# First transfers of a fused RWKV, soft-MoE and bilinear kernel put in another order, with four fewer warming matmuls

## The chip, the cores and the metric

The kernel runs on one core of a Trainium2 chip. The metric is the device time of one execution in microseconds, taken as the median of several runs.

## What is computed

Three layers follow one another in float32. The first is a linear attention with a decay per key channel (4 batches, 8 heads, 768 positions, 48 channels), the second a soft mixture of 8 experts with 4 slots each, the third a bilinear layer.

```python
def _attn_ref(r, k, v, w, u):
    state = np.zeros((B, H, D, D), dtype=np.float32)
    for t in range(S):
        kt, vt, rt, wt = (k[:, :, t], v[:, :, t], r[:, :, t], w[:, :, t])
        cur = np.einsum('bhd,bhe->bhde', u[None] * kt, vt)
        y[:, :, t] = np.einsum('bhd,bhde->bhe', rt, state + cur)
        state = wt[:, :, :, None] * state + np.einsum('bhd,bhe->bhde', kt, vt)

def _moe_ref(x, phi, w1, w2):            # x: 3072 x 384, 32 slots, inner width 1024
    logits = x @ phi
    slot_input = softmax_over_tokens(logits).T @ x
    for e in range(E):
        slot_out[e] = np.maximum(slot_input[e] @ w1[e], 0.0) @ w2[e]
    return softmax_over_slots(logits) @ slot_out

def _moe2_ref(x, w_a, w_b, w_out):       # inner width 1536
    return ((x @ w_a) * (x @ w_b)) @ w_out
```

The three matrices of the last layer are stored in float64. The kernel turns them into float32 with integer operations on ScalarE, VectorE and GpSimd.

## The kernel before

**Units.** The attention is cut into 16 units (`NU`). A unit is four heads over 384 positions of one batch, and the 384 positions are three chunks of 128. Units 0 and 1 are the two halves of the heads over the same positions, and so are 2 and 3, and so on. For every unit four inputs are loaded: w (the decays), k, r and v. `Chunked.load` (line 481) issues one such load as three DMAs on SyncE's queue, one for each chunk, 96 KB each, in pieces of 48 floats. SyncE issues its DMAs strictly in the order of the program, and a DMA whose destination is still being read waits there, with all that come behind it. In the text w1 means the decays of unit 1, k2 the keys of unit 2, and so on.

**Buffers.** w, k and r have one buffer each (`self.nat`), so the load for the next unit may start only when this unit has been turned; v has three. `front` (line 492) prepares a unit: `turn` (501) transposes w, k and r on TensorE, in two halves p = 0 and 1, and ScalarE copies them out of PSUM (L510 for w, L512 for k and r). `decays` (528) multiplies the decays up by a scan on VectorE (L529), `ends` takes a reciprocal (L538), `backward` (532) scans from the other end (L534), `key` and `query` multiply these into k and r (L547, L551). At the end of `turn` for k and r, and in `over` (541) for w, the load for unit n + 1 is issued into the buffer that has just become free. `over` itself is a ScalarE pass over w that sums how far it exceeds 1 (L543).

**A unit's second part.** `mid` (565) makes the masked scores: matmuls L579, masked on VectorE (L583). It turns the keys back (L591), updates the states (L599 on TensorE, L604 and L610 on VectorE) and makes the bonus term (L628 and after). `out` (662) makes the result of the unit (L672, L680, L683).

**Order of the work.** The schedule is written by hand: the order of the calls is the order on each engine. In the main loop over n (from line 1392) `run_all` weaves five streams by weights: `mid` of unit n, `front` of unit n + 1, `out` of unit n − 1, a piece of the expert layer, and a piece of `convert` (730), which makes float32 of the float64 matrices. The weaving places the turn of w for unit n + 1 between the key turn and the scores of unit n, and in the first round of `convert` two `stage` calls (701; ScalarE L704 and L705) come between the two halves p = 0 and p = 1 of the turn of w for unit 2.

**The start.** Fourteen matmuls on zeros (`WARM`, L1353) run on TensorE while the first loads are on their way. `Chunked.__init__` (426) issues w0, k0, r0, v0, the small tensor u and v1; `build_consts` (155) issues phi (L157); the front of unit 0 issues k1, w1, r1. Four float64 pieces of 384 KB (L723) are first loaded when `convert` is first called, in round 1 of the loop, behind v2. Later pieces follow one by one. Expert weights are loaded on the same queue (L773).

**The end.** After the attention the expert layer waits for its weights, and the bilinear layer follows; the change does not touch these.

Of the kernel before, what the change touches and what calls it, by code (L numbers as in the profile page):

```python
# [26 lines left out]
KEEP = (0, 0, 0, 0, 0, 0, 0, 0, 0, 0, 0, 0, 2, 4, 10, 2)  # L27
KEPT = 1
MOEW = (327, 327, 300, 200, 400, 0, 400)
WARM = 14  # L30
LATER = {6: 'more', 7: 'half', 9: 'more', 10: 'half'}
FEND = 0.53
CONV0 = 1
# [110 lines left out]
        self.NG = self.NT // self.G  # L144


def build_ident(nc, pool):
    ident = pool.tile([128, 128], F32, name="ident")
    nc.gpsimd.memset(ident, 1.0)
    nc.gpsimd.affine_select(out=ident, in_=ident, compare_op=ALU.is_equal, fill=0.0,  # L150
                            base=0, channel_multiplier=1, pattern=[[-1, 128]])
    return {"ident": ident}


def build_consts(nc, pool, sh, phi, k):
    phi_sb = pool.tile([128, sh.KB, sh.NS], F32, name="phi_sb")
    nc.sync.dma_start(out=phi_sb, in_=phi.rearrange("(k p) s -> p k s", p=128))  # L157
    k["phi"] = phi_sb
    ident = k["ident"]
    NS = sh.NS  # L160
    same = pool.tile([3 * NS, 4, NS], F32, name="same")
    for i in range(4):
        nc.gpsimd.tensor_copy(out=same[:, i, :], in_=ident[0:3 * NS, 0:NS])
    for i in range(1, 3):
        nc.gpsimd.tensor_copy(out=same[i * NS:(i + 1) * NS, :, :], in_=same[0:NS, :, :])
    k["same"] = same.rearrange("p c s -> p (c s)")
    half = pool.tile([128, 1], F32, name="half")
    nc.gpsimd.memset(half, 1.0)
    nc.gpsimd.memset(half[0:32], 0.5)
    k["half"] = half  # L170
    ones = pool.tile([128, 1], F32, name="ones")
    nc.gpsimd.memset(ones, 1.0)
    k["ones"] = ones
    zero = pool.tile([128, 1], F32, name="zero")
    nc.gpsimd.memset(zero, 0.0)
    k["zero"] = zero
# [233 lines left out]
class Chunked:  # L410
# [15 lines left out]
    def __init__(self, nc, sb, pool, sh, k, r, kk, v, w, u):  # L426
        self.nc, self.sh, self.k = nc, sh, k
        self.src = {"r": r, "k": kk, "w": w, "v": v}
        D = sh.D
        N = 6 * (C + 1)  # L430
        NP = sh.H // 2
        mask = sb.tile([128, C], F32, name="mask")
        nc.gpsimd.memset(mask, 1.0)
        nc.gpsimd.affine_select(out=mask, in_=mask, compare_op=ALU.is_gt, fill=0.0,
                                base=0, channel_multiplier=-1, pattern=[[1, C]])
        self.mask = mask
        lo = sb.tile([128, N // 2], F32, name="lo")
        nc.gpsimd.memset(lo, PLOW)
        nc.gpsimd.memset(lo[:, 0:N // 2:C + 1], 1.0)
        self.lo = lo  # L440
        neg1 = sb.tile([128, 1], F32, name="neg1")
        nc.vector.memset(neg1, -1.0)
        nc.scalar.activation(out=sb.tile([128, 1], F32, tag="neg"), in_=neg1, func=ACTF.Copy)
        self.neg1 = neg1
        self.nat = {}
        for nm, nb in (("w", 1), ("k", 1), ("r", 1), ("v", 3)):
            W = D if nm == "v" else 64
            self.nat[nm] = [sb.tile([128, 3, 4, W], F32, name="nat_" + nm + (str(i) if nm == "v" else ""))
                            for i in range(nb)]
            for t in self.nat[nm]:  # L450
                if W > D:
                    nc.gpsimd.memset(t[:, :, :, D:], 1.0 if nm == "w" else 0.0)
        for nm in "wkr":
            self.load(nm, 0)
        self.load("v", 0)
        u2 = sb.tile([128, NP, 32], F32, name="u2")
        nc.gpsimd.memset(u2, 0.0)
        uv = u.rearrange("(q hh) d -> hh d q", hh=2)
        for hh in range(2):
            nc.sync.dma_start(out=u2[64 * hh:64 * hh + D, :, hh], in_=uv[hh])  # L460
        self.u2 = u2
        self.load("v", 1)
        self.wt = sb.tile([128, N + 1], F32, name="wt")
        nc.gpsimd.memset(self.wt[:, 0:N + 1:C + 1], 0.0)
        self.d1 = sb.tile([128, N], F32, name="dl")
        nc.gpsimd.memset(self.d1, 0.0)
        self.sbd = [sb.tile([128, 2, 3, 2 * D], F32, name="sbd") for i in range(2)]
        for t in self.sbd:
            nc.gpsimd.memset(t, 0.0)
        nu = sh.NG * 2  # L470
        self.pc_all = pool.tile([128, nu, 6], F32, name="pc_all")
        self.wover = pool.tile([128, nu], F32, name="wover")
        self.T = [[sb.tile([128, 2, 3, D], F32, name="T") for i in range(2)] for q in range(2)]
        self.st = {}

    def unit(self, n):
        g, q = divmod(n, 2)
        b, hf = divmod(g, 2)
        return b, hf, q

    def load(self, nm, n):
        nc, D, G = self.nc, self.sh.D, self.sh.G
        if n >= 2 * self.sh.NG:
            return
        b, hf, q = self.unit(n)
        t = self.nat[nm][n % len(self.nat[nm])]
        for c in range(3):
            s = hf * G + c * C
            nc.sync.dma_start(out=t[:, c, :, 0:D],  # L489
                              in_=self.src[nm][b, 4 * q:4 * q + 4, s:s + C, :].rearrange("h p d -> p h d"))  # L490

    def front(self, n, sb, ps_t):
# [6 lines left out]
        pc = self.pc_all[:, n, :]  # L499

        def turn(nm, p):
            t = self.nat[nm][n % len(self.nat[nm])]
            pt = ps_t.tile([128, 3, C], F32, tag="tp", name="pt")
            for c in range(3):
                nc.tensor.transpose(out=pt[:, c, :],  # L505
                                    in_=t[:, c, 2 * p:2 * p + 2, :].rearrange("p h d -> p (h d)"),
                                    identity=ident)
            off = p * 3 * C
            if nm == "w":
                nc.scalar.activation(out=part(wt, p, 1), in_=pt, func=ACTF.Copy)  # L510
            else:
                nc.scalar.activation(out=(kT if nm == "k" else rT)[:, off:off + 3 * C],  # L512
                                     in_=pt.rearrange("p c s -> p (c s)"), func=ACTF.Copy)
            if p and nm != "w":
                self.load(nm, n + 1)
# [23 lines left out]
            nc.gpsimd.tensor_copy(out=pc, in_=P[:, C::C + 1])  # L539

        def over():
            t = self.nat["w"][0].rearrange("p c h d -> p (c h) d")[:, :, 0:self.sh.D]
            nc.scalar.activation(out=t, in_=t, func=ACTF.Relu, bias=self.neg1, accum_out=self.wover[:, n:n + 1])  # L543
            self.load("w", n + 1)

        def key(p):
            (nc.gpsimd if n else nc.vector).tensor_tensor(out=part(suf, p, 1), in0=part(suf, p, 1), in1=plain(kT, p),  # L547
# [182 lines left out]
def convert(nc, sb, jobs, n):  # L730

    raws = [load_f64(nc, sb, src, n) for src, _ in jobs[:RAWS]]
    stage(nc, jobs[0][1], raws[0])
    for i, (_, dst) in enumerate(jobs):
        if i + 1 < len(jobs):
# [457 lines left out]
def kernel(  # L1193
# [145 lines left out]
    with tc.manual_schedule(), ExitStack() as fast:  # L1339
# [49 lines left out]
        conv = convert(nc, sb, js, NH)  # L1389
        nconv = 4 * len(js)  # L1390
        early = wq.loads(NPRE)
        for n in range(NU + 1):
            streams = []
            if n < NU:
# [45 lines left out]
    with tc.If(val > 0):  # L1440
        with ExitStack() as slow:
# [8 lines left out]
                sb.add(slots.take(i), *Chunked.AREAS[i - NPRE])  # L1450
            k = build_ident(nc, pool)
            build_consts(nc, pool, sh, phi, k)
            moe = Moe(nc, pool, dp, sh, k)
            sb2 = Carve()
            siT = k["phi"]
# [48 lines left out]
```

## Time and profile before

| what | value |
|---|---|
| median of 3 runs | 389.91 us (389.46 to 389.98) |
| the profiled execution's own time | 389.08 us |
| its span, first to last instruction | 387.4 us |
| mean granted TensorE clock | 0.944 |
| busy: TensorE, VectorE, ScalarE, GpSimd | 87%, 78%, 59%, 46% of the span |
| moved by DMA | 73.75 MB, mean 190 GB/s |

The profile is of one execution. PE is TensorE's matmul part and PEld its weight load, DVE is VectorE, ACT ScalarE, POOL GpSimd, SP SyncE; a q behind a name is the queue of the engine, where it issues. Times count from the start of the span, which is 1.7 us shorter than the execution's own time. L505 is line 505 of the program printed above. The chain of waits follows the work back from the last instruction, each time to what released it.

### The profile page before, as it was taken

How to read it: one execution, taken by the hardware profiler on the slowest of the kernel's cores; microseconds unless marked ns; L12 is line 12 of the kernel's file. 1: busy time of each engine (PE TensorE's matmuls, PEld its weight loads, DVE VectorE, ACT ScalarE, POOL GpSimd, SP SyncE). 2: the span in 40 equal slices, each digit the busy share in tenths (PEclk: the TensorE clock that was granted, in tenths of full speed). 3: DMA queues.
4: the chain of work that ended last, by engine and by line, in shares of the span. 5: the costliest groups of instructions: out<-in, count | busy, mean ns of one | idle time of the engine just before them, and what ended most of it. 6: DMA issues, size and time to landing. Idle time of an engine off the chain costs nothing.

```text
span 387.4 us, 9985 instructions
## 1 busy us (share of the span) xinstructions
PE 336.3 (87%) x3634; PEld 265.7 (69%) x3634; DVE 303.2 (78%) x616; ACT 226.8 (59%) x672; POOL 179.3 (46%) x224
## 2 busy tenths in 40 slices
PE   8587979988878979878879888899998988999993
PEld 4365867766757858757757776654357867999993
DVE  2476999999999998999999995343519879887851
ACT  3275786785976958877768775234313235544451
POOL 5263766666675666765757761000006834222200
PEclk9697789999999879989989999899999999999998
DMA  7759687889979767989686989599929400899422
GB/s 124 126 111 267 152 195 209 185 164 237 243 148 236 172 129 201 225 198 213 153 174 155 240 278 311 192 330 377 368 81 217 92 0 2 229 277 301 146 89 70
DMA packets 138634, 73.75 MB, mean 190 GB/s; under 512 B 105328, under 2 KB 133104, under 8 KB 138576
## 3 DMA queue, kind: packets, MB, share of 16 engines
q1 hardware_dynamic: 137424, 69.48, 71.6%
q0 software_dynamic: 1152, 3.54, 2.8%
q8 instruction: 31, 0.51, 0.6%
q14 instruction: 27, 0.22, 0.2%
HBM read 67.68 MB, written 5.31 MB: 188 GB/s over the span
## 4 chain that ended last, share of the span: by engine, by line
DVE 51%; PE 23%; DMA 12%; issue 5%; SPq 4%; ACT 3%; POOL 0%; DVEq 0%; ACTq 0%; POOLq 0%
DVE s L534 8%; DVE s L529 8%; DMA s<-in_moe_w_dram 6%; DVE s L583 6%; PE yo L1103 6%; DVE s L712 5%; DVE s L551 4%; DVE wab L714 4%; PE tp L968 3%; PE yo L1106 3%; SPq L489 3%; DVE s L683 2%; DVE wo L714 2%; DVE s L610 2%; PE tp L579 2%
## 5 line engine op out<-in xcount | busy, mean ns | idle before, releaser
L505 PE MATMUL tp<-ident,s 128*128 128x128 f32 x288 | 49.5, 295 | 7.3 <-ACT s L593 3.6
L579 PE MATMUL tp<-s,s 64*128 64x128 f32 x384 | 38.6, 304 | 17.8 <-DVE s L610 9.5
L579 PEld LDWEIGHTS tp<-s,s 64*128 64x128 f32 x384 | 31.1, 201 | 23.1 <-issue 20.8
L554 POOL TENSOR_TENSOR s<-s,s 128x384 f32<-128x384 f32 x32 | 37.4, 1187 | 18.5 <-DVE s L551 18.5
L647 ACT ACTIVATE s<-s,s 128x48 f32<-128x48 f32 x192 | 45.6, 323 | 0.2
L505 PEld LDWEIGHTS tp<-ident,s 128*128 128x128 f32 x288 | 33.2, 147 | 17.3 <-issue 5.3
L547 POOL TENSOR_TENSOR s<-s,s 128x384 f32<-128x384 f32 x30 | 36.7, 1236 | 15.8 <-DVE s L534 10.0
L529 DVE TENSOR_TENSOR_SCAN s<-s,s 128x387 f32<-128x387 f32 x32 | 33.1, 1072 | 7.2 <-ACT s L510 7.2
L583 DVE TENSOR_TENSOR s<-tp,s 128x384 f32<-128x384 f32 x64 | 32.4, 545 | 7.8 <-PE tp L579 7.6
L1103 PE MATMUL yo<-s,s 128*128 128x384 f32 x192 | 38.1, 339 | 0.3 <-DVE s L1068 0.3
L534 DVE TENSOR_TENSOR_SCAN s<-s,s 128x387 f32<-128x387 f32 x32 | 35.0, 1121 | 0.5
L680 PEld LDWEIGHTS y<-s,s 128*64 128x64 f32 x768 | 29.0, 156 | 9.1 <-issue 8.8
L1103 PEld LDWEIGHTS yo<-s,s 128*128 128x128 f32 x192 | 33.7, 188 | 1.5 <-DVE s L1068 0.9
L680 PE MATMUL y<-s,s 128*64 128x48 f32 x768 | 33.3, 243 | 0.0
L512 ACT ACTIVATE s<-tp 128x384 f32<-128x384 f32 x64 | 30.2, 489 | 1.6 <-PE tp L505 0.6
L717 POOL TENSOR_TENSOR wab<-wab,s 128x384 int32<-128x384 int32 x24 | 27.9, 1160 | 6.3 <-DVE wab L714 2.8
L968 PE MATMUL tp<-s,s 128*128 128x384 f32 x144 | 27.3, 343 | 3.5 <-DVE s L954 3.2
L968 PEld LDWEIGHTS tp<-s,s 128*128 128x128 f32 x144 | 24.5, 188 | 7.1 <-DVE s L954 4.5
L1110 ACT ACTIVATE s<-yo 128x384 f32<-128x384 f32 x24 | 11.8, 493 | 27.8 <-PE yo L1107 14.4
L712 DVE TENSOR_SCALAR s<-s 128x384 uint32<-128x384 uint32 x36 | 23.2, 644 | 3.1 <-ACT wab L704 3.1
L1111 POOL DMA_DIRECT2D out_dram<-s x18 | 9.9, 550 | 33.8 <-ACT s L1110 31.9
L620 POOL TENSOR_TENSOR s<-s,pc_all 64x288 f32<-64x288 f32 (+1 forms) x32 | 21.2, 662 | 6.6 <-DVE s L610 5.4
(190 smaller groups left out, 733.0 us busy)
## 6 DMA issues: line engine op xcount, KB each, us to landing
s<-in_moe_w_dram SPq DMA_DIRECT2D x64, 384.0 KB, 6.1
s<-in_w_dram SPq DMA_DIRECT2D x48, 96.0 KB, 3.7
s<-in_k_dram SPq DMA_DIRECT2D x48, 96.0 KB, 4.6
s<-in_r_dram SPq DMA_DIRECT2D x48, 96.0 KB, 3.5
s<-in_v_dram SPq DMA_DIRECT2D x48, 96.0 KB, 3.4
s<-in_moe_w_a_dram SPq DMA_DIRECT2D x12, 384.0 KB, 4.1
s<-in_moe_w_b_dram SPq DMA_DIRECT2D x12, 384.0 KB, 3.6
s<-in_moe_w_out_dram SPq DMA_DIRECT2D x12, 384.0 KB, 3.6
```

The lines of the kernel that those rows point to most:

```text
L505: nc.tensor.transpose(out=pt[:, c, :], in_=t[:, c, 2 * p:2 * p + 2, :].rearrange("p h d -> p (h d)"), identity=ident)
L529: nc.vector.tensor_tensor_scan(out=P[:, hs[p]], data0=wt[:, hs[p]], data1=self.lo, initial=0.0, op0=ALU.mult, op1=ALU.max)
L534: nc.vector.tensor_tensor_scan(out=suf[:, hs[p]][:, ::-1], data0=wt[:, o + 1:o + H + 1][:, ::-1], data1=d1[:, hs[p]][:, ::-1], initial=0.0 ...
L547: (nc.gpsimd if n else nc.vector).tensor_tensor(out=part(suf, p, 1), in0=part(suf, p, 1), in1=plain(kT, p), op=ALU.mult)
L554: nc.gpsimd.tensor_tensor(out=plain(rT, p), in0=plain(rT, p), in1=plain(kT, p), op=ALU.mult)
L579: nc.tensor.matmul(out=aps[hh][:, c, :], lhsT=K[64 * hh:64 * hh + 64, o + 1:o + 1 + C], rhs=R[64 * hh:64 * hh + 64, o:o + C], start=True, ...
L583: nc.vector.tensor_tensor(out=a, in0=aps[hh], in1=self.mask.unsqueeze(1).to_broadcast([128, 3, C]), op=ALU.mult)
L647: nc.scalar.activation(out=av[:, c, h], in_=V[:, c, h, 0:D], func=ACTF.Copy, scale=a0[:, c, h // 2, h % 2:h % 2 + 1])
L680: nc.tensor.matmul(out=yp[th, c, hh, :], lhsT=am[p, hh][:, c, th], rhs=V[:, c, 2 * p + hh, :], start=False, stop=c == 2 and hh == 1)
L712: nc.vector.tensor_scalar(out=raw[:, :, 1], in0=raw[:, :, 1], scalar1=0x80000000, scalar2=None, op0=ALU.bitwise_and)
L968: nc.tensor.matmul(out=tp[m], lhsT=a[:, m * 128:(m + 1) * 128], rhs=b, start=first and i == 0, stop=last and i == 2)
L1103: nc.tensor.matmul(out=y, lhsT=a[:, m, :], rhs=self.th[:, m, :], start=m == 0 and a is fh, stop=False)
```

## The change

Five edits, all at the start of the program:

- The decays of unit 1 get a place of their own, `self.second`, in one of the two buffers that carry the tag "x", and are loaded right behind r0. `tile` says which place a unit's input has. GpSimd sets the unused columns of the new place (one more memset).
- `over` issues the load of w for unit n + 1 only from n = 2 on. The load of w2 is written ahead of the main loop, into the old buffer.
- `convert` gets a `yield` behind its first four loads, and is stepped once ahead of the main loop, so these four loads (384 KB each) stand in front of w2, k2, r2 and v2.
- v1 is issued behind the front of unit 0, phi behind w2.
- 10 warming matmuls in place of 14.

```diff
-WARM = 14
+WARM = 10
...
+def load_phi(nc, phi, k):
+    nc.sync.dma_start(out=k["phi"], in_=phi.rearrange("(k p) s -> p k s", p=128))
...
+        self.second = sb.tile([128, 3, 4, 64], F32, tag="x", name="nat_w1")
+        nc.gpsimd.memset(self.second[:, :, :, D:], 1.0)
         for nm in "wkr":
             self.load(nm, 0)
+        self.load("w", 1)
         self.load("v", 0)
...
-        self.load("v", 1)
...
+    def tile(self, nm, n):
+
+        return self.second if nm == "w" and n == 1 else self.nat[nm][n % len(self.nat[nm])]
...
-            t = self.nat["w"][0].rearrange("p c h d -> p (c h) d")[:, :, 0:self.sh.D]
+            t = self.tile("w", n).rearrange("p c h d -> p (c h) d")[:, :, 0:self.sh.D]
             nc.scalar.activation(out=t, in_=t, func=ACTF.Relu, bias=self.neg1, accum_out=self.wover[:, n:n + 1])
-            self.load("w", n + 1)
+            if n > 1:
+                self.load("w", n + 1)
...
     raws = [load_f64(nc, sb, src, n) for src, _ in jobs[:RAWS]]
+    yield 0
     stage(nc, jobs[0][1], raws[0])
...
         early = wq.loads(NPRE)
+        att.load("v", 1)
+        next(conv)
+        att.load("w", 2)
+        load_phi(nc, phi, k)
         for n in range(NU + 1):
```

`load` and `turn` now ask `tile` for the place, and `build_consts` only makes phi's buffer.

On SyncE's queue, the first loads before. A row is one load; in `s_2_76<-in_w_dram` the left side is the buffer and the right side the input.

```order
L489 DMA s_2_76<-in_w_dram 128x4x48 x3
L489 DMA s_2_79<-in_k_dram 128x4x48 x3
L489 DMA s_3_80<-in_r_dram 128x4x48 x3
L489 DMA s_6_92<-in_v_dram 128x4x48 x3
L460 DMA s_7_93<-in_u_dram 48x4x1 x2
L489 DMA s_3_83<-in_v_dram 128x4x48 x3
L157 DMA phi_sb<-in_moe_phi_dram 128x3x32
L489 DMA s_2_79<-in_k_dram 128x4x48 x3
L489 DMA s_2_76<-in_w_dram 128x4x48 x3
L489 DMA s_3_80<-in_r_dram 128x4x48 x3
```

The same place in the changed program:

```order
L497 DMA s_2_76<-in_w_dram 128x4x48 x3
L497 DMA s_2_79<-in_k_dram 128x4x48 x3
L497 DMA s_3_80<-in_r_dram 128x4x48 x3
L497 DMA s_7_93<-in_w_dram 128x4x48 x3
L497 DMA s_6_92<-in_v_dram 128x4x48 x3
L465 DMA s_7_93<-in_u_dram 48x4x1 x2
L497 DMA s_2_79<-in_k_dram 128x4x48 x3
L497 DMA s_3_80<-in_r_dram 128x4x48 x3
L497 DMA s_3_83<-in_v_dram 128x4x48 x3
```

w1 moved from ninth to fourth place, into the buffer `s_7_93`, and v1 went behind r1; phi left this part.

Still on SyncE's queue, the loads that follow, before (in_moe_w_a is the first float64 matrix, in_moe_w the expert weights):

```order
L489 DMA s_2_79<-in_k_dram 128x4x48 x3
L489 DMA s_2_76<-in_w_dram 128x4x48 x3
L489 DMA s_3_80<-in_r_dram 128x4x48 x3
L489 DMA s_4_87<-in_v_dram 128x4x48 x3
L723 DMA s_1_72<-in_moe_w_a_dram 128x768
L723 DMA s_1_73<-in_moe_w_a_dram 128x768
L723 DMA s_1_74<-in_moe_w_a_dram 128x768
L723 DMA s_1_75<-in_moe_w_a_dram 128x768
L773 DMA s_9_391<-in_moe_w_dram 128x3x256
```

And now:

```order
L732 DMA s_1_72<-in_moe_w_a_dram 128x768
L732 DMA s_1_73<-in_moe_w_a_dram 128x768
L732 DMA s_1_74<-in_moe_w_a_dram 128x768
L732 DMA s_1_75<-in_moe_w_a_dram 128x768
L497 DMA s_2_76<-in_w_dram 128x4x48 x3
L148 DMA phi_sb<-in_moe_phi_dram 128x3x32
L497 DMA s_2_79<-in_k_dram 128x4x48 x3
L497 DMA s_3_80<-in_r_dram 128x4x48 x3
L497 DMA s_4_87<-in_v_dram 128x4x48 x3
L783 DMA s_9_388<-in_moe_w_dram 128x3x256
```

The four float64 pieces went ahead of everything of unit 2, w2 went ahead of k2, and phi stands behind w2. On TensorE, VectorE, ScalarE and GpSimd the order of the work stays as it was, apart from the four matmuls less and the one memset more.

## Rows read from the trace of the kernel before

**Rows 1.** Busy time in stretches: us, busy (instructions) of PE, PEld, DVE, ACT, POOL; PEclk, DMA share, GB/s.

```profile
40.00:230.00 190.00, 164.94 (x2136) 132.50 (x2135) 185.31 (x378) 143.78 (x473) 125.87 (x134) 0.94 0.84 195
230.00:258.00 28.00, 24.39 (x331) 18.09 (x330) 13.33 (x51) 12.06 (x48) 2.65 (x7) 0.94 0.81 265
```

**Rows 2.** What VectorE waited for, 0 to 40 us: total, times, longest.

```profile
DVE s L529 <- ACT s L510: 7.2, 2, 6.7
DVE s L583 <- PE tp L579: 6.6, 2, 4.8
DVE s L712 <- ACT wab L704: 3.1, 1, 3.1
```

**Rows 3.** The chain of waits, 10 to 37 us: start, length, what.

```profile
13.26 3.19 DMA s<-in_w_dram
...
28.21 3.92 DMA s<-in_moe_w_a_dram
```

**Rows 4.** Timeline of SyncE's queue: start, length, instruction; x3 are a load's three DMAs.

```profile
2.40 1.61 SPq L489 DMA_DIRECT2D s<-in_k_dram  x3
...
7.41 0.92 SPq L460 DMA_DIRECT2D s<-in_u_dram  x2
8.38 1.54 SPq L489 DMA_DIRECT2D s<-in_v_dram  x3
...
28.21 1.93 SPq L723 DMA_DIRECT2D s<-in_moe_w_a_dram  x4
```

**Rows 5.** Timeline of TensorE, 0 to 36 us; the wait ahead of a row in brackets.

```profile
1.26 5.69 PE L1353 MATMUL tp<-s 128*128 128x512 bf16 x14 [1.26 <-DVE s L442]
...
6.79 2.26 PE L505 MATMUL tp<-ident,s 128*128 128x128 f32 x18
...
18.48 1.54 PE L505 MATMUL tp<-ident,s 128*128 128x128 f32 x6
...
26.03 0.30 PE L505 MATMUL tp<-ident,s 128*128 128x128 f32 x1
...
27.38 0.33 PE L505 MATMUL tp<-ident,s 128*128 128x128 f32 x1 [0.26 <-DMA s<-in_w_dram]
```

**Rows 6.** Timeline of ScalarE, 16 to 36 us.

```profile
27.75 0.49 ACT L510 ACTIVATE s<-tp 128x384 f32<-128x384 f32 x1 [0.79 <-PE tp L505]
32.15 0.54 ACT L704 ACTIVATE wab<-s 128x384 f32<-128x384 f32 x1 [3.91 <-DMA s<-in_moe_w_a_dram]
...
33.99 0.46 ACT L510 ACTIVATE s<-tp 128x384 f32<-128x384 f32 x1
```

**Rows 7.** Timeline of VectorE, 16 to 36 us.

```profile
18.58 1.02 DVE L583 TENSOR_TENSOR s<-tp,s 128x384 f32<-128x384 f32 x2 [4.85 <-PE tp L579]
...
28.61 1.02 DVE L583 TENSOR_TENSOR s<-tp,s 128x384 f32<-128x384 f32 x2 [1.77 <-PE tp L579]
32.72 0.36 DVE L712 TENSOR_SCALAR s<-s 128x384 uint32<-128x384 uint32 x1 [3.09 <-ACT wab L704]
33.00 0.96 DVE L529 TENSOR_TENSOR_SCAN s<-s,s 128x387 f32<-128x387 f32 x1
34.48 0.96 DVE L529 TENSOR_TENSOR_SCAN s<-s,s 128x387 f32<-128x387 f32 x1 [0.53 <-ACT s L510]
```

**Rows 8.** The four float64 loads from 28.2 to 29.7 us, issue to landing.

```profile
DMA to landing us min/median/max: 3.9/5.0/6.2
```

**Rows 9.** DMA issues of 20 to 28.2 us: count, KB each, median us to landing.

```profile
s<-in_w_dram SPq DMA_DIRECT2D x3, 96.0 KB, 3.0
```

**Rows 10.** The DMA issued from 31.1 to 31.2 us, the same columns.

```profile
s<-in_k_dram SPq DMA_DIRECT2D x1, 96.0 KB, 6.5
```

**Rows 11.** Busy time in stretches, the columns of rows 1.

```profile
13.50:14.00 0.50, 0.00 (x0) 0.00 (x0) 0.24 (x1) 0.47 (x1) 0.50 (x1) 0.50 0.81 158
20.00:26.00 6.00, 5.04 (x66) 3.94 (x66) 5.79 (x14) 5.71 (x21) 2.98 (x4) 1.00 0.48 90
31.00:31.50 0.50, 0.50 (x6) 0.40 (x4) 0.00 (x0) 0.00 (x0) 0.00 (x0) 1.00 0.94 369
```

**Rows 12.** The chain of waits, 225 to 262 us: the same twelve matmuls, twice.

```profile
232.07 1.31 PE y L672 x12
...
241.56 2.49 PE y L672 x12
```

More of the change, by code (lines that the diff above doesn't have):

```diff
@@ L155, in build_consts @@
 def build_consts(nc, pool, sh, phi, k):
-    phi_sb = pool.tile([128, sh.KB, sh.NS], F32, name="phi_sb")
-    nc.sync.dma_start(out=phi_sb, in_=phi.rearrange("(k p) s -> p k s", p=128))
-    k["phi"] = phi_sb
+    k["phi"] = pool.tile([128, sh.KB, sh.NS], F32, name="phi_sb")
     ident = k["ident"]
@@ L485, in load @@
         b, hf, q = self.unit(n)
-        t = self.nat[nm][n % len(self.nat[nm])]
+        t = self.tile(nm, n)
         for c in range(3):
@@ L501, in turn @@
         def turn(nm, p):
-            t = self.nat[nm][n % len(self.nat[nm])]
+            t = self.tile(nm, n)
             pt = ps_t.tile([128, 3, C], F32, tag="tp", name="pt")
@@ L1452 @@
             build_consts(nc, pool, sh, phi, k)
+            load_phi(nc, phi, k)
             moe = Moe(nc, pool, dp, sh, k)
```

## The prediction

> **What bounds the kernel now.** I read the busy time by stretches first, then VectorE's waits, then the chain of waits and the timelines of the first 36 us.
>
> From 40 to 230 us VectorE is busy 185.31 of 190 us [rows 1]. There it sets the pace; each unit's loads are released by the unit's own work, so the stretch starts when VectorE has its inputs and then runs its length. From 230 to 258 us TensorE carries the chain (24.39 of 28 us busy), and behind it the expert weights come in, issued as earlier work frees their places. So a microsecond won ahead of 40 us should be found again at the end, and VectorE's idle time ahead of 40 us is what there is to win. It stands in three lines [rows 2]: the scans wait for w to be turned (7.2 us, 6.7 of it at the very start), the masks wait for scores (6.6 in two pieces, 4.8 the longest), and the first float64 step waits 3.1 us for ScalarE.
>
> The chain says what stands behind two of them [rows 3]. The last third of w1, issued at 13.26, lands 3.19 later, at 16.45; TensorE's turn of w1 stands ahead of the scores in its order, so the scores and the masks (18.58) wait. And ScalarE, after half of w2, stands 3.91 us before L704 until the first float64 piece is there at 32.13 [rows 3, 6]; the other half of w2 is copied only behind two such steps (33.99), so the second scan of unit 2 starts at 34.48 [rows 7]. From there VectorE is full. I therefore work out when that scan starts in the changed kernel.
>
> **The queue.** A load of three takes 1.61 us and a gap of 0.05, u 0.92 and a gap [rows 4]; call it 1.65 and 0.97. k0 is at 2.40 and r0 at 4.05 as before. Then come w1 at 5.70, v0 7.35, u 9.00, k1 9.97, r1 11.62, v1 13.27, the four float64 pieces at 14.92 (1.93 before, so to 16.9), w2 at 16.90, phi 18.55, k2 19.1. The waits for a free buffer do not hold it up: k0 and r0 are turned by 9.05 (the 18 matmuls at 6.79 take 2.26 [rows 5]), before k1 and r1 are reached, and w0 is read long before w2's turn.
>
> **w1 early.** Its last third is issued at 6.8 and lands some 3.2 later, at 10.0 instead of 16.45. Before, from landing to masks it took 18.58 − 16.45 = 2.1 us; those stay, counted from the end of the key turn, so of the 4.85 us wait 2.7 go.
>
> **Four matmuls less.** 14 take 5.69 us [rows 5], so four are 1.6 us. The first turn of w0 follows right behind, and its DMAs have landed by then: the last is issued at about 1.9, and 3.0 to landing gives 4.9 [rows 9], against 6.79 − 1.6 = 5.2. So VectorE's first scan starts about 1.6 us earlier. r0 lands where it did (about 8.3), which is early enough for its use on VectorE some five microseconds behind the first scan. Together TensorE reaches the turn of w2 not at 26.03 [rows 5] but some 1.6 + 2.7 = 4.3 us earlier, at 21.7.
>
> What ten leave of the clock no run here shows. The 18 matmuls behind fourteen took 0.126 us each; six in a stretch granted 0.50, that is 1.2 GHz, took 0.257 [rows 5, 11]. At that level the first turns would be up to 2.4 us later, which is rival C. A rule speaks for it: the Trainium skill, "TensorE: Matmul & The Clock Gate", section "What's actually happening", has TensorE throttled by default, and activity releases the throttle. By it the shorter warming may leave the first turns at 1.2 GHz, and the time goes from the forecast towards C's; the trace agrees in so far as the granted clock is 0.50 behind the idle stretch ahead of 13.5 us.
>
> **Float64 pieces ahead of w2.** This is the step that decides. w2 stands behind four transfers of 384 KB. Before, those landed 3.9 to 6.2 us after their issue [rows 8], and a load of 96 KB behind five large ones took 6.5 us where others take 3.0 [rows 9, 10]; so they do go one behind the other. The last piece, issued at 16.4, lands at 22.6. w2's three thirds follow at the small pieces' rate, 96 KB at 158 GB/s or 0.62 us each [rows 11]: 24.5. The other way: 31.15 + 6.5 = 37.6 for the first third behind five, one large piece less (1.07 us at 369 GB/s) is 8.4 after the first issue, 14.92 + 8.4 + 2 × 0.62 = 24.5. So TensorE, there at 21.7, waits for w2 until 24.5, and this wait takes the place of the one for float64. It also swallows up to 2.8 us of anything late ahead of it: the slow level in the first turns, k1 (landing at about 14) and r1 (about 16), and GpSimd's one memset more, which is done long before u, at 9.00, needs the place behind it.
>
> **From w2 to the scan.** Before, TensorE took the last third at 27.38, the masks followed at 28.61 and ScalarE's copy at 27.75 [rows 5, 6, 7]. All of it 2.88 earlier: masks 25.73 to 26.75, copy 24.87 to 25.3. The first float64 piece has been there since 14.92 + 3.9 = 18.8, so L704 starts at 25.3; L712 could start 0.57 later, VectorE is free at 26.75, and the two scans follow at 27.05 and 28.0 (0.28 for L712, 0.96 for a scan). The second half of w2 is copied at 25.3 + 1.84 = 27.15 and done at 27.6, so it holds nothing up. The scan of 34.48 starts at 28.0: **6.5 us earlier**. k2, r2 and v2 follow w2 on the queue, partly waiting there for the large ones; r2 lands at about 27, ahead of the state updates, which come behind this scan, a reciprocal and two scans more on VectorE.
>
> v1 and phi cost nothing: v1 lands at about 17, its first use is in unit 1's updates, phi's in the expert layer from round 3 on.
>
> The profiled execution's own time is 389.08, so the sum gives 382.6. The median of the runs shown is 0.8 above it; on that scale I forecast **383.4 us**.
>
> **Rivals.**
>
> B, w2 is not late: the pieces spread so that w2 lands 3.0 after its issue (21.0). Then TensorE's arrival at 21.7 decides, another 2.5 us is won, 380.9; if the clock is also up in the stretch of 13.5 to 20 us, 379.9. Against it stands the 6.5 us row.
>
> C, the clock: the low level lasts through the start. 2.4 us in the first turns, and up to 5.04 more where TensorE was busy at granted 1.00 from 20 to 26 us [rows 11], less the 2.8 hidden: 0 to 4.6 us are lost, 383.4 to 388; I take 385.6. For it speaks that the clock was at 0.50 from 13.5 us on already; against it, that the long gaps of that time are cut.
>
> D, w2 later still: were the large pieces to go at the small ones' 158 GB/s, four take 10 us and w2 lands at 29.6, leaving 1.4 us, 388.5; half way, 386. The 369 GB/s speak against it.
>
> E, slower: the attention ends earlier, but TensorE's clock falls more often in the stretch from 230 to 258 us. There the same twelve matmuls took 1.31 and 2.49 us [rows 12], a ratio of 1.9 as between the two levels, and VectorE does not cover it. The kernel becomes slower than before when more than 6.5 us of full-level work there fall to 1.2 GHz; if 8 do, 391.4. The mean of 0.94 says that it is about 3 us now [rows 1]; a shift by 6.5 us changes where gaps fall, but not their number.
>
> F, no change: the win is given back in VectorE's long stretch by GpSimd running beside other steps. The 2% idle there leave little room.
>
> **How the numbers follow.** Forecast 0.62, B 0.13, C 0.08, D 0.08, E 0.05, F 0.04. The range takes the forecast with the bounds of its sum, B, and most of C and D: 379.8 to 387.0. A change of 0.2% (0.8 us) is about what a measurement of this kernel can tell from none. Faster: all of the first four, 0.91; same 0.04; slower 0.05.
>
> **What would show it.** L704 no longer waits for its DMA; the turn of w2 waits for one, of 2 to 4 us, landing at 24 to 25; the turn of w1 waits for none; the first scan starts at 6.1 to 6.6; unit 2's second scan at about 28; from there to the end the same distances as before. It is wrong if that scan comes at 28 and the span is not some 6 us shorter, or if the scan stays beyond 31.

## The result and the profile after

| | before | after |
|---|---|---|
| median of 4 runs each, us (lowest to highest) | 389.69 (387.78 to 389.98) | 381.80 (381.46 to 385.30) |
| ratio of the medians, 95% interval | | 0.9841 [0.9808, 0.9875] |
| profiled execution, its time / span, us | 389.08 / 387.4 | 381.9 / 380.2 |
| mean granted clock of TensorE | 0.944 | 0.948 |

The forecast was 383.4 us, in a range of 379.8 to 387.0, and faster; 381.80 lies in the range, and the interval of the ratio below 1. On the scale of the profiled execution it was 382.6 against 381.9 measured: 7.2 us won where 6.5 were forecast. The other 0.9 us of the distance to 381.80 is a matter of scale: the median of before lay 0.8 above its profiled execution, that of after lies 0.1 below.

Line numbers moved by 8 to 10: the turn of w is L513 (L505 before), ScalarE's copies of it L518 (L510), the float64 step L713 (L704), the scans L537 (L529), the masks L592 (L583).

SyncE's queue after, the timeline of its DMA issues (start, length, instruction), in the place of [rows 4]:

```profile
5.70 1.61 SPq L497 DMA_DIRECT2D s<-in_w_dram  x3
...
14.93 1.93 SPq L732 DMA_DIRECT2D s<-in_moe_w_a_dram  x4
16.95 1.63 SPq L497 DMA_DIRECT2D s<-in_w_dram  x3
...
19.64 4.25 SPq L497 DMA_DIRECT2D s<-in_k_dram  x3
```

The rows are w1, the float64 pieces, w2 and k2. The first three start within 0.05 us of the forecast, k2 0.5 later. k2's three issues take 4.25 us instead of 1.6: behind the large pieces the queue is held up, which the working had only as "partly waiting".

TensorE's timeline, beside [rows 5]:

```profile
1.26 4.45 PE L1363 MATMUL tp<-s 128*128 128x512 bf16 x10 [1.26 <-DVE s L444]
5.50 2.03 PE L513 MATMUL tp<-ident,s 128*128 128x128 f32 x13
...
20.62 0.87 PE L600 MATMUL tp<-ident,s 128*128 128x128 f32 x6
23.45 1.07 PE L513 MATMUL tp<-ident,s 128*128 128x128 f32 x3 [1.96 <-DMA s<-in_w_dram]
24.45 1.66 PE L588 MATMUL tp<-s,s 64*128 64x128 f32 x12
```

TensorE is done with what stands ahead of w2 at 21.5 (forecast 21.7) and then waits for w2. The last row is the score matmuls behind the turn. ScalarE beside [rows 6], and VectorE beside [rows 7]:

```profile
24.56 0.49 ACT L518 ACTIVATE s<-tp 128x384 f32<-128x384 f32 x1 [1.63 <-PE tp L513]
24.95 0.54 ACT L713 ACTIVATE wab<-s 128x384 f32<-128x384 f32 x1
```

```profile
6.98 1.82 DVE L537 TENSOR_TENSOR_SCAN s<-s,s 128x387 f32<-128x387 f32 x2 [5.76 <-ACT s L518]
...
14.11 1.02 DVE L592 TENSOR_TENSOR s<-tp,s 128x384 f32<-128x384 f32 x2 [1.30 <-PE tp L588]
...
26.14 1.02 DVE L592 TENSOR_TENSOR s<-tp,s 128x384 f32<-128x384 f32 x2 [3.77 <-PE tp L588]
27.08 0.35 DVE L721 TENSOR_SCALAR s<-s 128x384 uint32<-128x384 uint32 x1
27.34 1.81 DVE L537 TENSOR_TENSOR_SCAN s<-s,s 128x387 f32<-128x387 f32 x2
29.07 0.53 DVE L723 SCALAR_TENSOR_TENSOR wab<-wab,s 128x384 uint32<-128x384 uint32 x1
29.52 0.19 DVE L546 RECIPROCAL s<-s 128x6 f32<-128x6 f32 x1
```

L713 follows the copy with no wait for a DMA: the 3.91 us of [rows 3, 6] are gone. Unit 0's masks stand at 14.11 instead of 18.58. The second half of the two scans in the row at 27.34 starts at about 28.2; it was 34.48. The wait that is left is that of the masks at 26.14, 3.77 us, and the chain of waits of the changed kernel (start, length, what) names what is behind it:

```profile
1.26 4.45 PE tp L1363 x10
...
16.95 6.37 DMA s<-in_w_dram
23.45 1.07 PE tp L513 x3
24.52 1.58 PE tp L588 x12
```

w2, first issued at 16.95, lands 6.0 to 6.4 us after each issue, where a load of that size took 3.0 [rows 9]. So the wait for w2 has taken the place of the wait for float64, as forecast. Stretches after, in the columns of rows 1; the last two are those of [rows 1], each 6.8 to 7 us earlier:

```profile
22.00:24.00 2.00, 0.55 (x2) 0.36 (x2) 0.37 (x1) 0.93 (x3) 1.93 (x4) 0.84 0.58 91
24.00:30.00 6.00, 6.00 (x40) 5.07 (x39) 3.83 (x8) 3.23 (x7) 1.24 (x3) 0.50 0.91 177
...
33.20:223.20 190.00, 165.31 (x2121) 131.05 (x2123) 185.22 (x379) 144.96 (x476) 126.21 (x134) 0.93 0.84 196
223.00:251.00 28.00, 24.39 (x354) 18.27 (x350) 14.01 (x52) 11.95 (x47) 3.11 (x8) 0.97 0.83 275
```

VectorE's long stretch holds the same 185.2 us of work and the stretch behind it the same 24.39 on TensorE: nothing was given back there.

**Where the 7.2 us are.** VectorE takes one reciprocal of six numbers per unit (L546 above), in unit 2 some 1.3 us behind the start of the second scan; its start is a mark that every run has. The table has that of units 2, 3 and 15 (the last), and the end, of the profiled execution of each run.

| run | unit 2 | unit 3 | unit 15 | end | median, us (runs) | ratio to before beside it |
|---|---|---|---|---|---|---|
| before | 35.81 | 49.15 | 222.84 | 387.4 | 389.69 (4) | |
| after | 29.52 | 42.86 | 216.47 | 380.2 | 381.80 (4) | 0.9841 [0.9808, 0.9875] |
| e1, after again | 29.51 | 42.86 | 216.18 | 380.8 | 381.91 (6) | 0.9843 [0.9819, 0.9866] |
| e9, after again | 28.98 | 42.31 | 216.85 | 382.4 | 383.24 (6) | 0.987 [0.9829, 0.9911] |
| e2, 14 warming | 29.38 | 42.72 | 216.94 | 379.6 | 381.66 (6) | 0.9844 [0.9817, 0.987] |
| e5, w1 alone | 32.25 | 45.56 | 220.58 | 384.0 | 385.81 (12) | 0.9937 [0.9912, 0.9962] |
| e4, float64 late | 30.92 | 44.25 | 217.66 | 382.8 | 383.79 (6) | 0.989 [0.9853, 0.9928] |
| e7, two more large | 31.82 | 45.16 | 217.84 | 382.4 | 384.78 (9) | 0.9912 [0.9882, 0.9942] |
| e6, no second place | 30.61 | 43.94 | 217.06 | 381.0 | 384.72 (6) | 0.9895 [0.9849, 0.9941] |
| e12, the same again | 30.43 | 43.77 | 216.93 | 380.9 | 384.10 (6) | 0.9902 [0.9873, 0.9931] |
| e3, w2 first | 28.09 | 42.21 | 216.81 | 381.2 | 382.85 (6) | 0.9855 [0.9822, 0.9888] |
| e8, w2 first, 6 warming | 26.80 | 42.25 | 214.91 | 378.7 | 381.37 (6) | 0.9835 [0.9788, 0.9882] |
| e11, pieces 2 and 2 | 27.30 | 40.63 | 213.29 | 378.2 | 380.02 (6) | 0.9798 [0.9756, 0.9839] |
| e10, the same, 6 warming | 26.53 | 39.95 | 213.47 | 377.2 | 378.92 (5) | 0.9767 [0.9738, 0.9796] |

From before to after unit 2's mark moves by 6.29, unit 15's by 6.37, and the end by 7.2. The last 0.8 us come behind the attention, where the chain's first wait for expert weights is 8.28 us instead of 9.48. The repeats show no effect of the change there: from unit 15's mark to the end it is 163.73 in after, but 164.62 and 165.55 in the two other profiled executions of the same program, and 164.56 before. The medians scatter as well: beside the kernel before, the same change won 7.9, 6.3 and 4.5 us (after, e1, e9).

### The profile page after: what moved, and what is told of

The parts are those of the page before. It is cut to its first block, busy times and chain, and to the rows that moved or that the text cites. A ratio compares the mean times of both kernels' runs of the same rounds, so it can differ in the third digit from the quotient of the medians.

```text
span 380.2 us, 9979 instructions
## 1 busy us (share of the span) xinstructions
PE 334.0 (88%) x3630; PEld 264.1 (69%) x3630; DVE 303.0 (80%) x616; ACT 226.9 (60%) x672; POOL 179.7 (47%) x225
## 3 DMA queue, kind: packets, MB, share of 16 engines
q0 software_dynamic: 1152, 3.54, 2.8%
## 4 chain that ended last, share of the span: by engine, by line
DVE 48%; PE 30%; DMA 11%; issue 5%; ACT 3%; SPq 1%; POOL 0%; DVEq 0%; ACTq 0%; POOLq 0%
DVE s L542 8%; DVE s L537 7%; PE yo L1113 7%; DMA s<-in_moe_w_dram 6%; DVE s L592 6%; DVE s L721 5%; DVE wab L723 4%; DVE s L560 3%; PE tp L978 3%; PE yo L1116 3%; PE tp L588 3%; DVE s L692 2%; PE y L689 2%; DVE wo L723 2%; PE tp L513 2%
## 5 line engine op out<-in xcount | busy, mean ns | idle before, releaser
L513 PE MATMUL tp<-ident,s 128*128 128x128 f32 x288 | 49.7, 297 | 8.6 <-ACT s L602 5.2
L513 PEld LDWEIGHTS tp<-ident,s 128*128 128x128 f32 x288 | 33.5, 148 | 19.4 <-ACT s L602 8.6
L588 PEld LDWEIGHTS tp<-s,s 64*128 64x128 f32 x384 | 31.1, 202 | 20.8 <-issue 18.3
L592 DVE TENSOR_TENSOR s<-tp,s 128x384 f32<-128x384 f32 x64 | 32.4, 545 | 7.6 <-PE tp L588 7.6
L537 DVE TENSOR_TENSOR_SCAN s<-s,s 128x387 f32<-128x387 f32 x32 | 32.4, 1054 | 5.8 <-ACT s L518 5.8
L926 POOL TENSOR_TENSOR s<-s 128x512 f32<-128x512 f32 x11 | 13.8, 1254 | 20.3 <-DMA s<-ct 13.6
## 6 DMA issues: line engine op xcount, KB each, us to landing
s<-in_moe_w_dram SPq DMA_DIRECT2D x64, 384.0 KB, 5.9
s<-in_moe_w_a_dram SPq DMA_DIRECT2D x12, 384.0 KB, 4.2
s<-in_moe_w_b_dram SPq DMA_DIRECT2D x12, 384.0 KB, 3.7
s<-in_moe_w_out_dram SPq DMA_DIRECT2D x12, 384.0 KB, 3.7
```

Of the source, the lines that this page charges most:

```text
L513: nc.tensor.transpose(out=pt[:, c, :], in_=t[:, c, 2 * p:2 * p + 2, :].rearrange("p h d -> p (h d)"), identity=ident)
L537: nc.vector.tensor_tensor_scan(out=P[:, hs[p]], data0=wt[:, hs[p]], data1=self.lo, initial=0.0, op0=ALU.mult, op1=ALU.max)
L588: nc.tensor.matmul(out=aps[hh][:, c, :], lhsT=K[64 * hh:64 * hh + 64, o + 1:o + 1 + C], rhs=R[64 * hh:64 * hh + 64, o:o + C], start=True, ...
L592: nc.vector.tensor_tensor(out=a, in0=aps[hh], in1=self.mask.unsqueeze(1).to_broadcast([128, 3, C]), op=ALU.mult)
```

## Experiments

e1 to e4 ran beside each other, and so did e5 to e8 and e9 to e12. Before had a median of 388.22, 388.67 and 387.72 us in the three groups.

### e1: the changed kernel again

No edit.

> The changed kernel again, beside the three others on one chip. The theory on record (the landing of w2 sets the start of VectorE's long stretch, and the gain passes to the end): about 382 us, unit 2's second scan at 28.2 us, the three waits for expert weights on the chain together between 24 and 25 us. Rival (the 0.9 us won behind 28 us was chance): those waits come back to the 25.1 us of the kernel before, and the time is 382.5 or more.

Measured: 381.91 us, 0.9843, and the mark of unit 2 at 29.51, the same as in the first profile (second scan at 28.2). The first scan starts at 6.50, half a microsecond before that of after. It makes no difference from unit 2 on, because the wait for w2 covers it. The three waits for expert weights are 23.9 us together, a little less than expected (24.2 in after, 25.1 before); yet from unit 15 to the end e1 takes 164.62 us, as long as before. So it is not these waits alone that make the end longer or shorter.

e9 is the same program once more, in the third group, where 381.5 to 382.5 us and the second scan at 28.2 were expected. The median is 383.24 us, its six times lie between 381.65 and 385.41, and the second scan comes at 27.7: 1.3 us slower than e1 in the median, though unit 2 is earlier.

### e2: fourteen warming matmuls

```diff
-WARM = 10
+WARM = 14
```

> The changed kernel with 14 warming matmuls. Theory (the wait for w2 swallows what is late ahead of it): the first scan about 0.9 us later, at 7.9, the turn of w2 reached some 1 us later but still before w2 has landed at 24, so the time is that of the changed kernel within 0.5 us. Rival (the four matmuls lie on the path to the end): slower than the changed kernel by 0.9 to 1.7 us.

Measured: 381.66 us, no difference. But the first scan, expected at 7.9, was not late at all, as TensorE's timeline of this run shows:

```profile
1.26 4.70 PE L1363 MATMUL tp<-s 128*128 128x512 bf16 x14 [1.26 <-DVE s L444]
5.80 1.64 PE L513 MATMUL tp<-ident,s 128*128 128x128 f32 x13
...
23.36 1.03 PE L513 MATMUL tp<-ident,s 128*128 128x128 f32 x3 [0.33 <-DMA s<-in_w_dram]
```

Fourteen took 4.70 us here, against 5.69 for the same fourteen in [rows 5] and 4.45 for ten in after. The first scan starts at 6.92, where ten had it at 6.98. Unit 1's scan is 0.9 later than in after (15.92 against 15.04), behind a granted clock of 0.79 and 0.50 from 10 to 14 us where after had 1.00 and 0.78, and TensorE then waits 0.33 for w2 instead of 1.96: the cover was used, and w2 decides as before. What used it was work at the low clock, and not the four matmuls; that these cost nothing, the medians alone say.

### e5: w1's own place alone

The kernel before with the second place, w1's load behind r0, `tile`, and no load of w1 in `over`; everything else as before (14 warming matmuls, float64 behind v2, w2 behind k2).

```diff
+        self.second = sb.tile([128, 3, 4, 64], F32, tag="x", name="nat_w1")
+        nc.gpsimd.memset(self.second[:, :, :, D:], 1.0)
...
+        self.load("w", 1)
         self.load("v", 0)
...
-            self.load("w", n + 1)
+            if n:
+                self.load("w", n + 1)
```

> The kernel before with one part of the change: w1 in a place of its own, loaded behind r0; 14 matmuls, w2 and the float64 pieces where they were. Theory (w1's late landing cost 2.7 us, the float64 wait follows it): masks of unit 0 some 2.7 us earlier, unit 2's second scan at 31 to 32 instead of 34.5, ScalarE's wait for float64 still 3.5 to 4.5 us, time 2.5 to 3.5 us below the kernel before. Rival (w1 alone is hidden behind the float64 wait): less than 1 us.

Measured: 385.81 us, 2.9 less than before beside it. VectorE's timeline of this run:

```profile
14.85 1.02 DVE L591 TENSOR_TENSOR s<-tp,s 128x384 f32<-128x384 f32 x2 [2.19 <-PE tp L587]
...
30.92 0.96 DVE L536 TENSOR_TENSOR_SCAN s<-s,s 128x387 f32<-128x387 f32 x1 [0.51 <-ACT s L517]
```

The wait for w1 goes (masks at 14.85 instead of 18.58), the scan of 34.48 comes to 30.92, and ScalarE still waits for float64, 3.37 us in this run. So a single wait removed gives its part, and the other one stays. Of the 3.6 us at unit 2, 1.1 are not the place's: this execution's fourteen matmuls took 4.62 us, and its first scan started at 6.83 instead of 7.91.

### e4: the float64 pieces back behind v2

```diff
     raws = [load_f64(nc, sb, src, n) for src, _ in jobs[:RAWS]]
-    yield 0
...
         att.load("v", 1)
-        next(conv)
         att.load("w", 2)
```

> The changed kernel with the four float64 pieces back behind v2, w2 still early. Theory: w2 lands at 18 and is not waited for, but ScalarE waits for the first piece until about 26, the second scan comes at about 28, and the time is that of the changed kernel within 1 us: loading the pieces early buys nothing in this order. Rival (the early float64 pieces are the gain): the wait of 3.9 us is back in full, and the time is 3 to 4 us above the changed kernel.

Measured: 383.79 us, 1.9 more than e1 beside it. ScalarE's timeline shows the old wait back in its full length:

```profile
27.24 0.54 ACT L713 ACTIVATE wab<-s 128x384 f32<-128x384 f32 x1 [4.52 <-DMA s<-in_moe_w_a_dram]
```

But w2 is now there in time (copied at 22.24 instead of 24.56), so the wait starts earlier, and only 1.41 us are lost at unit 2's mark. They are found at unit 15 (1.48), and 1.9 in the median: more than the 1 us that I had given this step at most, and less than the rival's 3 to 4. Taking the three together, against before beside each: w1's place 2.9, then w2 ahead of k2 with the small moves to 4.4, then the float64 pieces to 6.3. The moves of v1 and phi were not tried by themselves.

### e7: two more large transfers ahead of w2

Two expert loads of 384 KB, which come later anyway, are issued between the float64 pieces and w2.

```diff
         next(conv)
+        next(early)
+        next(early)
         att.load("w", 2)
```

> The changed kernel with two of the expert weights' 384 KB loads moved between the float64 pieces and w2. Theory (each microsecond that w2 lands later is one at the end): w2 lands 2.2 us later, at about 26.3, the second scan comes at about 30.4, and the time rises by 2.2 us. Rival (w2 has slack, or transfers share the engines so that two more make no difference): less than 0.7 us.

Measured: 384.78 us. The ratio is 0.0069 above that of e1, or 2.7 us, though e1 ran in another group. TensorE's timeline of this run:

```profile
20.66 0.87 PE L600 MATMUL tp<-ident,s 128*128 128x128 f32 x6
25.85 0.97 PE L513 MATMUL tp<-ident,s 128*128 128x128 f32 x3 [4.33 <-DMA s<-in_w_dram]
```

TensorE arrives when it did in after (20.66 against 20.62) and waits 2.4 us longer. w2 is first issued 1.0 us later (17.96) and lands 6.4 to 7.8 us after each issue. 768 KB in 2.4 us is 330 GB/s, near the 369 of [rows 11]: the transfers go one behind the other, and each large one ahead of w2 costs 1.2 us. The end pays for it, 2.7 us in the medians; in the profiled execution 2.3 us at unit 2's mark and 1.7 at unit 15's, against e1. This settles the step that I had said decides, and rules out rival B, under which w2 lands 3.0 us after its issue.

### e6 and e12: no place of its own for w1

The changed kernel without the second place: w1 goes behind k1 and w2 behind k2, into the old buffer; the float64 pieces stay early.

```diff
-        self.second = sb.tile([128, 3, 4, 64], F32, tag="x", name="nat_w1")
-        nc.gpsimd.memset(self.second[:, :, :, D:], 1.0)
...
-        self.load("w", 1)
...
-            if n > 1:
-                self.load("w", n + 1)
+            self.load("w", n + 1)
...
-        att.load("w", 2)
```

> The changed kernel without the second place: w1 and w2 again in one buffer, w1 behind k1, w2 behind k2; the float64 pieces stay early. Theory: w1 lands at about 14.3, which costs little, but w2 now stands behind the float64 pieces and behind k2, whose three DMAs took until 23.9 to be issued; w2 lands at 27 to 28, the second scan comes at 31 to 32, and the time is 3 to 4 us above the changed kernel. Rival (the early float64 pieces alone are the gain, the place is not needed): within 1 us of the changed kernel.

> The sixth run again, since its times spread over 4.7 us: w1 and w2 in one buffer, the float64 pieces early. Its profile had the second scan 1.1 us later than the changed kernel. If that passes to the end, the time is 1 to 2 us above the changed kernel beside it; if the place of its own is worth nothing, the two agree within 0.5 us.

Measured: 384.72 and 384.10 us. In e6 unit 2's second scan is at 29.3, where I had expected 31 to 32: masks of unit 0 come at 16.43, 2.3 later than in after, but unit 2's mark only 1.1 later. TensorE's timeline of e6 shows how:

```profile
25.01 0.30 PE L510 MATMUL tp<-ident,s 128*128 128x128 f32 x1 [1.20 <-DMA s<-in_w_dram]
25.46 0.33 PE L510 MATMUL tp<-ident,s 128*128 128x128 f32 x1 [0.15 <-DMA s<-in_w_dram]
26.00 0.33 PE L510 MATMUL tp<-ident,s 128*128 128x128 f32 x1 [0.20 <-DMA s<-in_w_dram]
26.25 0.94 PE L584 MATMUL tp<-s,s 64*128 64x128 f32 x12
```

Here w2 stands behind k2 as well, and TensorE has its last third only 1.9 us later than in after, at 26.0 where I had expected it to land at 27 to 28. The twelve score matmuls behind it then take 0.94 us, in after 1.66, which gives 0.7 us of that back. Between after, e1 and e9 on one side and e6 and e12 on the other the mark of unit 2 differs by 0.9 to 1.6 us, that of unit 15 by 0.1 to 0.9, and e12's median is 0.9 above e9's, with intervals that overlap. So with the float64 pieces early the second place is worth about a microsecond at the start; what is left of it at the end these runs don't settle. The shares of the parts depend on the order in which they are taken: without the place, the rest of the change is worth 4.0 and 3.6 us (e6 and e12 against before beside them), and the place by itself was worth 2.9 in e5.

### e3: w2 ahead of the float64 pieces

```diff
         att.load("v", 1)
-        next(conv)
         att.load("w", 2)
+        next(conv)
         load_phi(nc, phi, k)
```

> The changed kernel with w2 issued ahead of the four float64 pieces. Theory (w2 waits behind those pieces, one transfer after the other): w2 lands at about 18 us, TensorE turns it on arrival at about 21.5 without a wait, unit 2's second scan starts at 25 to 26 instead of 28.2, and the time falls by 2 to 3 us, to about 379.5. Rival (k2 and r2 are late next, or the float64 pieces are again what ScalarE waits for): the scan comes at 27 or later and the time falls by less than 1 us.

Measured: 382.85 us, not faster than e1, where I expected 2 to 3 us less. The wait for w2 is gone, and unit 2's mark is 1.42 earlier than in e1 (its second scan at 26.8, where 25 to 26 were expected); at unit 3 0.65 is left of that, and at unit 15 nothing. The chain of this run between 14 and 34 us shows what is late in w2's place:

```profile
21.04 5.92 DMA s<-in_k_dram
```

k2's last third now stands behind the pieces and lands at 26.96. TensorE's keys of unit 2 wait for it, and the clock falls behind that (stretches of e3):

```profile
24.00:26.00 2.00, 0.97 (x11) 0.61 (x7) 1.67 (x4) 2.00 (x6) 1.70 (x3) 1.00 0.71 111
26.00:28.00 2.00, 1.62 (x9) 1.27 (x10) 2.00 (x3) 0.94 (x3) 0.15 (x1) 0.89 0.87 165
28.00:30.00 2.00, 2.00 (x18) 1.40 (x18) 1.97 (x4) 0.27 (x2) 1.92 (x2) 0.50 0.75 148
```

### e8: the same, with six matmuls on zeros behind the turn of r0

Besides e3's edit, six more warming matmuls, meant to keep the clock up until unit 0's gates. They compute nothing that is used.

```diff
+        wp = ps.tile([128, 512], F32, tag="A", name="wp2")
+        for _ in range(6):
+            nc.tensor.matmul(out=wp, lhsT=wz[:, 0:128], rhs=wz, start=True, stop=True)
```

> w2 ahead of the float64 pieces as in the third run, and six matmuls on zeros behind the turn of r0, where TensorE had 2.4 us without work. Theory (the third run lost part of its gain because the granted clock fell to 0.50 from about 11 to 17 us): the clock stays at 1.00 until 20 us, the turn of w2 comes at 21.3, the second scan at 25.6 to 26, unit 3's reciprocal at 41.5 or earlier (42.2 in the third run), and the time is 380 to 381. Rival (what is won ahead of 28 us is lost again in the units behind, whatever the clock does early): 382 or more.

Measured: 381.37 us. The clock stays at 1.00 until 18 us and is 0.50 from 20 to 22. Unit 2's mark comes at 26.80, 1.3 earlier than in e3, and unit 3's at 42.25, where e3 has it too and where 41.5 or earlier was expected. VectorE's timeline of e8:

```profile
26.80 0.18 DVE L546 RECIPROCAL s<-s 128x6 f32<-128x6 f32 x1
27.01 2.59 DVE L542 TENSOR_TENSOR_SCAN s<-s,s 128x387 f32<-128x387 f32 x2
31.70 0.21 DVE L613 COPY s<-tp 128x48 f32<-128x48 f32 x1 [2.10 <-PE tp L608]
```

The copies of the states wait 2.1 us for TensorE, which had k2 at 26.20, 0.8 earlier than in e3, and ran at 0.50 from 26 to 32 us. Two runs, two starts, one mark at unit 3: what w2 first wins at unit 2 is mostly lost within that unit, as long as k2 comes behind four large pieces. At the end neither run shows a gain clear of the scatter: 382.85 and 381.37 us, against 381.91 and 383.24 for the changed kernel in e1 and e9.

### e10: two float64 pieces early, two behind v2

w2 goes first, then two of the four pieces, then phi, k2, r2 and v2, and the other two behind them; e8's six matmuls stay.

```diff
-    raws = [load_f64(nc, sb, src, n) for src, _ in jobs[:RAWS]]
+    raws = [load_f64(nc, sb, src, n) for src, _ in jobs[:2]]
     yield 0
+    raws += [load_f64(nc, sb, src, n) for src, _ in jobs[2:RAWS]]
```

> As the eighth run (w2 first, six matmuls behind the turn of r0), but only two of the four float64 pieces ahead of unit 2's loads, the other two behind v2. Theory (in the eighth run k2, 5.1 us from issue to landing behind four large pieces, held up TensorE and with it the clock, and gave back 2.1 of the 2.7 us between unit 2 and unit 3): k2 lands by 23.5, unit 2's second scan at 25 to 25.6, unit 3's reciprocal at 40 to 41 instead of 42.25, the time 1 to 2.5 us below the changed kernel beside it. Rival (the long stretch gives it back anyway): within 0.7 us of the changed kernel.

Measured: 378.92 us (378.68 to 379.95), 8.8 less than before beside it and 4.3 less than e9, the changed kernel beside it (381.65 to 385.41). It beats both kernels. Its queue and its chain:

```profile
18.13 2.47 SPq L497 DMA_DIRECT2D s<-in_k_dram  x3
20.69 2.76 SPq L497 DMA_DIRECT2D s<-in_r_dram  x3
23.50 1.60 SPq L497 DMA_DIRECT2D s<-in_v_dram  x3
25.14 0.99 SPq L732 DMA_DIRECT2D s<-in_moe_w_a_dram  x2
```

```profile
20.14 3.98 DMA s<-in_k_dram
28.34 6.02 DMA s<-in_w_dram
```

The 4.3 us are more than the 1 to 2.5 expected, and in part they are e9's, whose median is 1.3 to 1.4 above those of e1 and after; the profiled executions differ by 3.0 from after. k2 lands at 24.12 instead of e3's 26.96, and unit 3 keeps what unit 2 wins: 2.99 against after at unit 2, 2.91 at unit 3, 3.00 at unit 15 and at the end. The next pinch is the chain's second row: w3, 6.02 us behind the other two pieces and an expert load.

### e11: the same without the six matmuls

> The same without the six matmuls. Theory: the granted clock falls to 0.50 somewhere between 10 and 17 us, the second scan comes about 1 us later than with them, and the time is 0.5 to 1.5 us above that of the run with them. Rival (the clock of the start costs nothing): the same within 0.4 us.

Measured: 380.02 us, 1.1 more than e10, about what I had given the clock; but not where I had. The granted clock did not fall at 10 to 17 us as in e3 and e9. It fell later, as the stretches show, of e11 and then of e10:

```profile
18.00:20.00 2.00, 0.72 (x10) 0.66 (x10) 1.86 (x8) 1.97 (x10) 2.00 (x2) 1.00 0.91 294
20.00:22.00 2.00, 2.00 (x13) 1.81 (x10) 1.96 (x4) 1.77 (x7) 1.50 (x3) 0.58 1.13 259
22.00:24.00 2.00, 2.00 (x16) 1.55 (x15) 0.08 (x1) 1.85 (x5) 1.93 (x3) 0.57 0.53 95
```

```profile
18.00:20.00 2.00, 0.66 (x10) 0.66 (x10) 1.86 (x8) 1.97 (x11) 2.00 (x2) 1.00 0.90 277
20.00:22.00 2.00, 1.86 (x15) 1.34 (x12) 1.96 (x4) 2.00 (x9) 1.51 (x3) 1.00 1.11 271
22.00:24.00 2.00, 1.98 (x16) 1.33 (x15) 1.22 (x3) 2.00 (x6) 1.93 (x3) 1.00 0.61 108
```

The 0.77 us that this costs at unit 2 are no longer there at unit 15, where e11 is 0.18 ahead. The 1.0 us at the end arise behind unit 15, where e11 takes 1.2 us longer: 0.5 of them ahead of the end of the chain's third wait for expert weights (273.93 in e11, 273.62 in e10), and the rest behind it. So the gain of the split is shown, by both runs; a gain of the six matmuls is not.

## Why the prediction was right, step by step

**What bounds.** That a microsecond ahead of 40 us is found again at the end held, to within a microsecond or so. From unit 2's mark to unit 15's it is 187.03 us before and 186.95 after, and 186.0 to 187.9 in the other runs but three. The three are e8 and e3 (188.1 and 188.7), which lost 2.1 and 0.8 us within unit 2, and e5 (188.3). What e5 lost, and the rest in e3, lies behind unit 3's mark: from there to unit 15's the runs take 172.7 to 175.0 us, and no run gives the cause of that scatter.

**The queue** was right to 0.13 us up to w2 (k1 at 10.10 for 9.97 is the worst). What it lacked is that k2 would be held up behind w2; in the changed kernel TensorE has no wait for k2, in e3 it has.

**w1 early** was right in kind: no wait for it, and masks at 14.11. Of the 4.47 us by which these came earlier, 0.93 is the first scan's start, which leaves 3.54 for w1 where 2.7 was forecast; the same reckoning gives 2.65 in e5. That TensorE reached w2 at 21.5 for 21.7 is partly luck: in this execution w1's term came out larger than forecast, and the next one smaller.

**Four matmuls less** was the term that was mis-sized: 1.6 us forecast, 0.9 measured at the first scan (6.98 against 7.91, where the forecast had 6.1 to 6.6). The step failed in dividing 5.69 us by fourteen. The price of a warming matmul is not the same from run to run: fourteen took 5.69, 4.70 and 4.62 us (before, e2, e5), ten 4.45, 4.29 and 3.93 (after, e1, e7). With fourteen the first scan started at 7.91, 6.92 and 6.83, with ten at 6.98 in eight runs and at 6.50, 6.48 and 6.15 in three, so even the 0.9 is mostly the one late execution of before. The Trainium skill, "TensorE: Matmul & The Clock Gate", section "What's actually happening", says that the same kernel measures different counts of matmuls at the low level from run to run. These rows agree in so far as the total varies; the counts they do not show. The mis-sizing cost the forecast nothing, because w2's wait covers it, as the working said it would: e2, with all fourteen, is no slower.

**Float64 ahead of w2** was right in kind and in size: forecast 24.5 for w2's landing, and TensorE took the last third at about 24.1. e7 shows the mechanism by itself. The Trainium skill, "DMA: Bandwidth & Descriptors", section "Queues, rings and completion order", has each DMA engine take the descriptors of a ring in order; the 6.0 to 6.4 us of w2, and the 6.4 to 7.8 in e7, agree with that.

**From w2 to the scan** I forecast masks at 25.73 and the scan at 28.0, from w2 at 24.5; measured were 26.14 and 28.2, from a w2 that was 0.4 earlier. So 0.6 to 0.8 us were lost between. The step took the durations of [rows 5], at granted 1.00; but behind the new wait the clock is 0.50 from 24 to 30 us, and there the twelve score matmuls take 1.66 us. In the kernel before and in e9, at 1.00, they took 0.94:

```profile
27.64 0.94 PE L579 MATMUL tp<-s,s 64*128 64x128 f32 x12
```

```profile
24.63 0.94 PE L588 MATMUL tp<-s,s 64*128 64x128 f32 x12
```

That is rival C's mechanism, at another place and for less than it was priced at. In e9, where TensorE waited 1.0 us for w2 instead of 1.96, the clock stayed at 1.00, and unit 2's mark is 0.54 earlier, though TensorE had w2's last third 0.3 later. The wait by itself does not decide the clock: e2 waited 0.33 and had 0.50 behind it too.

**The rivals.** B is ruled out by w2's 6.0 to 6.4 us and by e7. D is too: w2 came no later than forecast. C did not come in the first turns: thirteen of them took 2.03 us, 0.16 each, where C had 0.26. Its low level came later, from 14 to 16 us and from 24 to 30. E did not happen: the stretch of 28 us has the same 24.39 us of TensorE, at 0.97 instead of 0.94. F did not either: 185.22 against 185.31 us of VectorE in 190.

**The rest.** The forecast's sum lacked 0.7 us of the profiled time. Against the working, the start gave 0.2 us less than forecast and the part behind unit 15 0.8 more; the latter is luck, the scatter of that part, from 162.7 to 165.6 us over the fourteen profiled executions, and not the change.

## What to carry to other kernels

When loads share a queue, count the bytes ahead of each one, not its place: w2 was 6.4 us on its way behind four pieces of 384 KB, and moving it ahead only handed the wait to the next load, k2. Split what can be split, so that the loads which a unit needs stand between the large pieces, and follow the win over a whole unit before it is counted: e8 lost most of it within one unit, and e3 half. A term that lies under a longer wait (the warming here) needs no exact price, but the wait that covers it must be named and sized.

## What the runs showed of the hardware that was not expected

The clock does not follow from the idle time just ahead of it alone. In e10 and e11 TensorE is busy 0.66 and 0.72 us between 18 and 20 us, and the granted clock of the next 4 us is 1.00 in the one and 0.58 in the other; the two programs differ only in e10's six matmuls at 9 us. The same program had 0.50 from 12 to 16 us in e9; after had 0.78 and 0.50 there.

The granted clock column does not show the level of the first matmuls: it is 1.00 from 0 to 10 us in after, where ten warming matmuls take 0.445 us each, and six of the same shape take 1.46 us, 0.24 each, at 8.98 in e8. A first stretch must be read by the duration of its instructions.

DMA issues on SyncE wait as well. Three of 96 KB take 1.6 us, but 4.25 behind the large pieces in after and 4.57 for r2 in e3, without a wait on any buffer that the working found.
